# A summand for the fast matrix scheme, formed in place in its PSUM bank

## The chip, the core and the metric

The kernel runs on one core of a Trainium2 chip. Its engines work side by side: TensorE (PE; its weight loads are listed apart as PEld), VectorE (DVE), ScalarE (ACT) and GpSimd (POOL); SyncE issues the DMAs. Each engine executes its own queue in order, and waits for other engines by semaphores. The metric is the device time of one execution in microseconds (us).

## The reference

An attention layer is followed by two feed-forward layers (the setup of the inputs is left out):

```python
def _attn_ref(q, k, v, w1, b1, w2):          # q, k, v: 2 x 8 x 576 x 64
    ...
    scores = scale * np.matmul(q, k.transpose(0, 1, 3, 2))
    ...
    scores = scores + bias.transpose(2, 0, 1)[None, :, :, :]
    attn = softmax(scores)                    # exp, and division by the row's sum
    return np.matmul(attn, v)

def _moe_ref(x, w_gate, w_val, w_out):        # x: 1152 x 512, d_ff 1536
    g = x @ w_gate
    return (silu(g) * (x @ w_val)) @ w_out

def _moe2_ref(x, w_in, w_out):                # d_ff 2048
    return softplus(x @ w_in) @ w_out
```

The bias comes from a small network on the distance of two positions. All is float32.

## The kernel before

**Precision.** Products with full precision are made from two parts: a tensor's high part h is its value rounded to TensorE's format fp32r, its low part l is what is left (value minus h). Tiles with h or l at the end of the name are such parts.

**The feed-forward layers** (from line 640) multiply 2 x 2 blocks by a scheme with seven products instead of eight. The right-hand factor is the attention output, transposed and cut into blocks by head pairs and batches: B11 (head pairs 0 and 1, batch 0), B12 (the same, batch 1), B21 and B22 (head pairs 2 and 3). The scheme wants, beside the blocks, four sums: T1 = B12 − B11, T2 = B22 − T1, T3 = B22 − B12 and T4 = B21 − T2. All of them are kept as h and l.

**The attention** is done in eight units, one for each head pair and batch, in the order of `UNITS`: B11, B12 for head pair 0, B11, B12 for head pair 1, then B22 and B21. A unit has two parts (`sub`): the first with 256 query rows, the second with 320. A part has four or five chunks of scores. The function `run_slot` issues one chunk per slot, in a fixed order on all engines: TensorE makes the scores of the chunk (`scores`, tile ps, two buffers); finished parts are entered in a list (`finish`); copies of transposed blocks are made (`gather`, line 412, tiles at from pt); VectorE adds the bias to the scores and finds the row minima (`biased`, line 354); ScalarE takes the exp of the chunk before (`softmax`, line 368), VectorE sums and inverts (lines 372 and 375) and GpSimd scales (line 378); then pending preparations of queries and keys go on (`prep`, lines 189 to 195: h and l of Q and K, tiles qh, ql, kst); then `advance(late)` carries every finished part one step on; then TensorE transposes blocks (line 405). When all blocks of a part are copied, its value products run (`values`, line 432) in one go at the end of a slot, and the part is finished from the next slot on. They accumulate in the tile po, one PSUM bank; its pool has a single buffer:

```python
psO = pool("psO", 1, space=PSUM)     # line 622
```

**The end of a part** is the generator `finish` (line 440). Every `yield` without a value puts it off by a slot; `yield BLOCK` puts it off until the next part has issued its value products. For B12 it reads: ScalarE copies po to b12 (line 463); VectorE subtracts the high part of B11 from po into t1f, a place in SBUF that the bias no longer needs (line 464, by the helper of line 452, which is the line that the profile shows for every subtraction); behind a BLOCK, VectorE subtracts the low part of B11 from t1f, in place (line 466); a slot later ScalarE rounds t1f to T1h (line 468); behind one or two more BLOCKs VectorE makes T1l from t1f and T1h (line 472). t1f and b12 are read later, when B22 is finished (lines 476 and 477). So B12 goes through four such ends, two parts for each of the head pairs 0 and 1. In the trace, t1f and b12 carry the name bias, since they lie in a tile of the bias.

Of the kernel before, what the change touches and what calls it, by code (L numbers as in the profile page):

```python
# [44 lines left out]
BLOCK = "block"  # L45
# [58 lines left out]
def tile_kernel(ctx: ExitStack, tc, qT, kT, vS, vT, wg, wv, wo, wi, wo2, table, out):  # L104
    nc = tc.nc
# [11 lines left out]
    def slots(pool, tag, names):  # L117

        for name in names:
            n = len([1 for t in SLOTS.values() if t[0] == tag])  # L120
            SLOTS[name] = (tag, [pool.tile([P, 2, S], F32R, tag=f"{tag}{2 * n + i}", name=f"{name}{t}") for i, t in enumerate("hl")])

    def opener(stack):
        return lambda name, bufs, **k: stack.enter_context(
            tc.tile_pool(name=name, bufs=bufs, reuse_waits="tile", **k)
        )

    rctx = ExitStack()
    with ExitStack() as actx:
# [310 lines left out]
        def finish(u):  # L440

            if u["i"] == 2 and u["sub"] == 0:
                slots(xp, "a", ("B21", "B22"))
            if u["i"] == 4 and u["sub"] == 0:
                right.close()
                SLOTS["rp8"] = (None, opener(rctx)("rp8", 1, side="right"))
                slots(SLOTS["rp8"][1], "r", ("T2", "T3", "T4"))
            pr, sub, po = u["pr"], u["sub"], u["po"]
            n = 320 if sub else 256
            cols = slice(256 * sub, 256 * sub + n)  # L450
            po = po[:, :n]
            minus = lambda o, a, b, eng=nc.vector: eng.tensor_tensor(o, a, b, op=ALU.subtract)  # L452
            at = lambda name: [t[:, pr % 2, cols] for t in SLOTS[name][1]]
            floats = lambda name: [t.bitcast(F32) for t in at(name)]
            name = f"B{1 + pr // 2}{1 + u['b']}"
            if name != "B12":
                nc.scalar.copy(at(name)[0], po)
            k = pr % 2
            home = bias[1][:, 2 * k : 2 * k + 2, cols]
            t1f, b12 = home[:, 0], home[:, 1]  # L460
            chains = []
            if name == "B12":
                nc.scalar.copy(b12, po)
                minus(t1f, po, floats("B11")[0])
                yield BLOCK
                minus(t1f, t1f, floats("B11")[1])
                yield
                nc.scalar.copy(at("T1")[0], t1f)
                yield BLOCK
                if sub:  # L470
                    yield BLOCK
                minus(at("T1")[1], t1f, floats("T1")[0])
                return
            elif name == "B22":
                t2, t3 = t2f[:, k, cols], tmpp.tile([P, 320], F32, name="t")[:, :n]
                minus(t2, po, t1f)
                minus(t3, po, b12)
                chains = [("T2", t2), ("T3", t3)]
            elif name == "B21":
                t4 = tmpp.tile([P, 320], F32, name="t")[:, :n]  # L480
                minus(t4, po, t2f[:, k, cols])
                chains = [("T4", t4)]
            if not u["eager"]:
                yield
            if name != "B12":
                minus(at(name)[1], po, floats(name)[0])
            if u["eager"]:
                yield
                yield
            for to, t in chains:  # L490
                nc.scalar.copy(at(to)[0], t)
                yield
                minus(at(to)[1], t, floats(to)[0], nc.vector if u["eager"] else nc.gpsimd)
# [27 lines left out]
        def run_slot():  # L521
# [31 lines left out]
            for w in done:  # L553
                w["eager"] = slot >= len(chunks) - 1
                late.append(finish(w))
                if w["eager"]:
                    next(late[-1])
# [103 lines left out]
    def as_float(n):  # L661


        x = cvp.tile([P, 2 * NK, P], F32, tag="x", name="x")
        load(2 * n + 3)
        for j in range(2):
            raw, y = loaded[2 * n + j], x[:, NK * j : NK * (j + 1)]
            hw, lw, yi = raw[:, :, :, 1], raw[:, :, :, 0], y.bitcast(I32)
            if n < NL2:
                nc.scalar.activation(y, hw.bitcast(F32), AF.Prelu, scale=2.0**-112, alpha=-(2.0**32))  # L670
            else:
                nc.scalar.activation(y, hw.bitcast(F32), AF.Copy, scale=2.0**-112)  # L672
            nc.vector.tensor_scalar(yi, yi, 3, None, op0=ALU.logical_shift_left)  # L673
            if n >= NL2:
                nc.vector.scalar_tensor_tensor(yi, hw, -(2**31), yi, op0=ALU.bitwise_and, op1=ALU.bitwise_or)
            nc.vector.scalar_tensor_tensor(yi, lw, 29, yi, op0=ALU.logical_shift_right, op1=ALU.bitwise_or)  # L676
            load(2 * n + j + 4)
        return x
# [38 lines left out]
    class Quad:  # L717
# [8 lines left out]
        def floats(self):  # L726
            self.x = as_float(self.n)
# [129 lines left out]
    with tc.manual_schedule(engines={E.PE}):  # L857
# [118 lines left out]
        for m, order in ((2, (0, 1, 2)), (3, (2, 0, 1))):  # L976
            pt = [wide()[:, 0] for _ in TB]
            for fbs in [order[:1], order[1:]] if m == 3 else [(fb,) for fb in order]:
                at = {fb: blocks.index((m, fb)) for fb in fbs}
# [171 lines left out]
```

## Time and profile before

| | |
|---|---|
| Time, median of 3 runs | 587.55 us (587.5 to 587.6) |
| Profiled execution, span from first to last instruction | 585.8 us |
| Mean granted clock of TensorE | 1.000 of full speed |
| TensorE busy | 575.7 us (98%) |
| VectorE busy | 454.2 us (78%) |
| ScalarE busy | 374.8 us (64%) |
| GpSimd busy | 98.4 us (17%) |
| Line 452 on VectorE, second subtraction (bias<-bias,B11l) | 4 instructions, 81.5 to 130.0 us |
| Line 452 on VectorE, T1l | 4 instructions, 91.6 to 146.6 us |

The profiled execution's own time is given by its span alone. The attention fills the stretch from about 60 to 186 us; bias and first scores stand ahead of it, the feed-forward layers behind it. Times in a timeline are counted from the first instruction. A "part" below is one part of a unit as above; what is behind it in brackets in a row is the engine's idle time and the instruction that ended it, as far as the semaphores tell.

### The profile page before, as it was taken

What the parts mean: (1) busy time and instruction counts of PE and PEld (TensorE: products, weight loads), DVE (VectorE), ACT (ScalarE), POOL (GpSimd) and SP (SyncE); (2) the same over time, 40 slices, a digit from 0 to 9 for tenths busy, and PEclk for the clock granted to TensorE, in tenths of its full rate; (3) what the DMA queues carried; (4) which work ended last, traced back from release to release, by engine and by line L of the source; (5) the groups of instructions that cost most, each with busy time, mean ns of one, the idle gap of its engine ahead of it and who ended that gap; (6) DMA issues with size and microseconds to landing.
All of it is one profiled execution on the core that took longest, in us unless ns stands there. A gap on an engine that the chain in (4) does not pass through costs nothing.

```text
span 585.8 us, 11304 instructions
## 1 busy us (share of the span) xinstructions
PE 575.7 (98%) x4270; PEld 506.2 (86%) x4270; DVE 454.2 (78%) x970; ACT 374.8 (64%) x713; POOL 98.4 (17%) x151
## 2 busy tenths in 40 slices
PE   8999999999999999999999999999999999999997
PEld 5334588888887999999999999999989989989985
DVE  7999688888988998977879626579998877974332
ACT  8999888888787857656568325359727715733610
POOL 1002578888861000000000000000000000000000
PEclk9999999999999999999999999999999999999999
DMA  8999633233233342332343231322243241300012
GB/s 312 208 208 221 153 94 128 81 107 112 72 115 113 99 143 74 108 109 73 108 130 124 75 113 46 106 94 73 83 162 117 73 143 38 108 36 1 2 62 99
DMA packets 41894, 63.30 MB, mean 108 GB/s; under 512 B 4080, under 2 KB 30704, under 8 KB 41840
## 3 DMA queue, kind: packets, MB, share of 16 engines
q1 hardware_dynamic: 41840, 62.59, 36.1%
q8 instruction: 33, 0.54, 0.4%
q14 instruction: 21, 0.17, 0.1%
HBM read 49.60 MB, written 2.36 MB: 89 GB/s over the span
## 4 chain that ended last, share of the span: by engine, by line
PE 83%; DVE 7%; ACT 5%; DMA 3%; POOL 1%; issue 1%; DVEq 0%; ACTq 0%; POOLq 0%
PE pw L751 38%; PE pw L1059 17%; PE pw L702 13%; PE po L432 5%; PE pt L405 4%; PE ps L333 4%; DMA bias<-early 2%; PE ps L306 2%; ACT r L260 1%; PE pb L270 1%; ACT early L282 1%; DVE e L354 1%; DVE r L262 1%; DVE bias L354 1%; DVE T1l L452 1%
## 5 line engine op out<-in xcount | busy, mean ns | idle before, releaser
L1059 PE MATMUL pw<-oh,g2h 128*128 128x512 f32 x144 | 56.2, 390 | 0.0
L1059 PE MATMUL pw<-oh,g2l 128*128 128x512 f32 x144 | 56.2, 390 | 0.0
L1059 PE MATMUL pw<-ol,g2h 128*128 128x512 f32 x144 | 56.1, 390 | 0.0
L702 PE MATMUL pw<-gl,sh 128*128 128x384 f32 x144 | 48.2, 335 | 0.0
L702 PE MATMUL pw<-gh,sl 128*128 128x384 f32 x144 | 48.2, 334 | 0.0
L702 PE MATMUL pw<-gh,sh 128*128 128x384 f32 x144 | 48.2, 334 | 0.0
L262 DVE TENSOR_SCALAR r<-G 128x576 f32<-128x576 f32 x108 | 47.2, 522 | 0.1
L676 DVE SCALAR_TENSOR_TENSOR x<-raw,x 128x512 int32<-128x512 int32 x68 | 46.3, 688 | 0.9
L270 PE MATMUL pb<-r,G 128*32 128x288 f32 x576 | 44.4, 414 | 2.1
L378 POOL TENSOR_SCALAR e<-e,sm 128x576 f32<-128x576 f32 x44 | 33.8, 776 | 65.7 <-DVE sm L375 59.2
L270 PEld LDWEIGHTS pb<-r,G 128*32 128x32 f32 x576 | 18.8, 110 | 26.8 <-ACT early L282 15.1
L354 DVE CUSTOM_DVE_ANT_0 e<-ps,bias 128x576 f32<-128x576 f32 x44 | 33.0, 750 | 11.4 <-PE ps L333 6.6
L412 ACT COPY at<-pt 128x512 f32<-128x512 f32 (+2 forms) x69 | 36.4, 548 | 6.5 <-PE pt L405 6.1
L333 PE MATMUL ps<-kst,ql 128*128 128x288 f32 x120 | 36.9, 336 | 1.4 <-DVE sm L372 0.7
L432 PE MATMUL po<-at,v 128*64 128x256 f32 (+3 forms) x384 | 37.3, 332 | 1.0 <-DVE at L412 0.8
L1097 DVE TENSOR_TENSOR acc<-pw,acc 128x512 f32<-128x512 f32 x27 | 17.5, 685 | 25.1 <-PE pw L1059 25.1
L368 ACT ACTIVATE e<-e,sm 128x576 f32<-128x576 f32 x44 | 34.3, 781 | 3.5 <-DVE sm L354 3.0
L673 DVE TENSOR_SCALAR x<-x 128x512 int32<-128x512 int32 x68 | 28.8, 428 | 9.7 <-ACT x L672 5.0
L432 PEld LDWEIGHTS po<-at,v 128*64 128x64 f32 x384 | 26.8, 137 | 8.5 <-issue 1.7
L1059 PEld LDWEIGHTS pw<-oh,g2l 128*128 128x128 f32 x144 | 27.0, 188 | 5.8
L333 PE MATMUL ps<-kst,qh 128*128 128x288 f32 x120 | 32.0, 295 | 0.0
L681 ACT CAST oh<-x 128x512 fp32r<-128x512 f32 x16 | 9.9, 619 | 34.1 <-PE pw L1059 33.7
(270 smaller groups left out, 1684.3 us busy)
## 6 DMA issues: line engine op xcount, KB each, us to landing
raw<-in_wo_dram SPq DMA_DIRECT2D x28, 512.0 KB, 3.4
bias<-early SPq DMA_DIRECT2D x32, 288.0 KB, 8.1
raw<-in_wi_dram SPq DMA_DIRECT2D x16, 512.0 KB, 4.1
raw<-in_wv_dram SPq DMA_DIRECT2D x12, 512.0 KB, 4.6
raw<-in_wg_dram SPq DMA_DIRECT2D x12, 512.0 KB, 3.5
qr<-in_qT_dram SPq DMA_DIRECT2D x7, 576.0 KB, 3.7
bias<-in_kT_dram SPq DMA_DIRECT2D x6, 576.0 KB, 4.4
v<-in_vS_dram SPq DMA_DIRECT2D x8, 384.0 KB, 3.2
```

Source lines behind the costliest of these rows:

```text
L262: nc.vector.tensor_scalar(r, G[:, w0 : w0 + S], PB[:, n : n + 1], 0.0, op0=ALU.add, op1=ALU.max)
L270: nc.tensor.matmul(pb[32 * ct : 32 * ct + 32, hf, :HALF], W2, rs[ct][:, HALF * hf : HALF * (hf + 1)], start=True, stop=True,)
L333: nc.tensor.matmul(ps[:, hf, :HALF], u[t][:, o : o + P], kst[:, a, HALF * hf : HALF * (hf + 1)], start=i == 0, stop=i == len(parts) - 1,)
L354: nc.vector.tensor_tensor_reduce(out=e[:, :S].rearrange("p (a n) -> p a n", a=2), in0=ps[:, :, :HALF], in1=bt.rearrange("p (a n) -> p a n" ...
L368: nc.scalar.activation(e, e, AF.Exp, bias=sm[:, 0, n : n + 1], scale=-1.0, accum_out=u["sums"][:, n, :1])
L378: nc.gpsimd.tensor_scalar(e, e, sm[:, 2, i : i + 1], 1.0, op0=ALU.mult, op1=ALU.mult)
L412: marks[eng, u["i"], u["sub"]] = copy(at[:, :w], pt[:, :w]).ins
L432: nc.tensor.matmul(u["po"][D * a : D * (a + 1), o : o + n], v[:, D * t : D * (t + 1)], at[:, i : i + n], start=piece == 0 and o == 0, stop ...
L676: nc.vector.scalar_tensor_tensor(yi, lw, 29, yi, op0=ALU.logical_shift_right, op1=ALU.bitwise_or)
L702: nc.tensor.matmul(ps[:, :n], w[:, k], x, start=first and k == 0 and i == 0, stop=last and k == NK - 1 and i == 2)
L751: nc.tensor.matmul(ps[:, hf, :HALF], a[:, o + k], b[:, HALF * hf : HALF * (hf + 1)], start=start and k == 0 and i == 0, stop=k == 1 and i ...
L1059: nc.tensor.matmul(ps, g, w.rearrange("p k f -> p (k f)"), start=f == 0 and i == 0, stop=f == 3 and i == 2)
```

## The change

For B12 both subtractions of B11 now write their result back into po. They are made in two successive slots, without a BLOCK. Directly behind the second one ScalarE makes two copies out of po: T1h and the plain sum t1f. In the slot after that VectorE makes T1l from po and T1h. VectorE has as many subtractions as before; ScalarE has one copy more for each end, four in all.

```diff
@@ -460,16 +460,15 @@
             t1f, b12 = home[:, 0], home[:, 1]
             chains = []
             if name == "B12":
+                high11, low11 = floats("B11")
                 nc.scalar.copy(b12, po)
-                minus(t1f, po, floats("B11")[0])
-                yield BLOCK
-                minus(t1f, t1f, floats("B11")[1])
+                minus(po, po, high11)
                 yield
-                nc.scalar.copy(at("T1")[0], t1f)
-                yield BLOCK
-                if sub:
-                    yield BLOCK
-                minus(at("T1")[1], t1f, floats("T1")[0])
+                minus(po, po, low11)
+                nc.scalar.copy(at("T1")[0], po)
+                nc.scalar.copy(t1f, po)
+                yield
+                minus(at("T1")[1], po, floats("T1")[0])
                 return
```

The order of the instructions on VectorE and ScalarE moves with it; TensorE's does not.

VectorE, end of B12's second part for head pair 1, from the slot behind the one with the first subtraction; bias_72 holds t1f, bias_71 to bias_84 elsewhere are bias tiles or exp tiles, sm and sums the row statistics. Before:

```order
L372 TENSOR_REDUCE sm_101<-sums_105 128x1
L375 RECIPROCAL sm_101<-sm_101 128x1
L191 CAST qh<-qr 128x320
L412 COPY at<-pt 128x512
L354 ISA bias_82,sm_102<-ps,bias_71 128x576
L354 ISA sm_102 128x1
L372 TENSOR_REDUCE sm_102<-sums_106 128x1
L375 RECIPROCAL sm_102<-sm_102 128x1
L354 ISA bias_83,sm_102<-ps,bias_72 128x576
L354 ISA sm_102 128x1
L452 TENSOR_TENSOR T1l<-bias_72,T1h 128x256
L452 TENSOR_TENSOR bias_72<-bias_72,B11l 128x320
```

The two subtractions at the end stand a slot behind the value products; T1l (128x256) belongs to the part before. After:

```order
L372 TENSOR_REDUCE sm_101<-sums_105 128x1
L375 RECIPROCAL sm_101<-sm_101 128x1
L191 CAST qh<-qr 128x320
L452 TENSOR_TENSOR po<-po,B11l 128x320
L412 COPY at<-pt 128x512
L354 ISA bias_82,sm_102<-ps,bias_71 128x576
L354 ISA sm_102 128x1
L372 TENSOR_REDUCE sm_102<-sums_106 128x1
L375 RECIPROCAL sm_102<-sm_102 128x1
L452 TENSOR_TENSOR T1l<-po,T1h 128x320
L354 ISA bias_83,sm_102<-ps,bias_72 128x576
```

The second subtraction (128x320) has moved up to stand ahead of the copy of line 412, and T1l of the same part stands behind the next sum and reciprocal.

ScalarE, the same place, from the plain copy of po on; T1h is the high part of T1, at a copy of a transposed block. Before:

```order
L463 COPY bias_72<-po 128x320
L412 COPY at<-pt 128x512 x2
L368 ACTIVATE e_116,sums_105<-e_116,sm_101 128x576
L368 ACTIVATE bias_82,sums_106<-bias_82,sm_102 128x576
L189 CAST qh<-qr 128x320
L412 COPY at<-pt 128x256
L368 ACTIVATE bias_82,sums_106<-bias_82,sm_102 128x576
L412 COPY at<-pt 128x512
L368 ACTIVATE bias_83,sums_106<-bias_83,sm_102 128x576
L468 CAST T1h<-bias_72 128x320
```

Six instructions stand between the exp of e_116 and T1h. After:

```order
L464 COPY bias_72<-po 128x320
L412 COPY at<-pt 128x512 x2
L368 ACTIVATE e_116,sums_105<-e_116,sm_101 128x576
L468 CAST T1h<-po 128x320
L469 COPY bias_72<-po 128x320
L368 ACTIVATE bias_82,sums_106<-bias_82,sm_102 128x576
L189 CAST qh<-qr 128x320
L412 COPY at<-pt 128x256
L368 ACTIVATE bias_82,sums_106<-bias_82,sm_102 128x576
```

T1h and the plain sum stand directly behind that exp, ahead of the exp of bias_82 and the cast of the queries.

VectorE, end of B12's first part for head pair 1; kst are the parts of K of the next unit. Before:

```order
L191 CAST kst<-bias_71 128x576
L354 ISA e_115,sm_101<-ps,bias_82 128x576
L354 ISA sm_101 128x1
L195 TENSOR_TENSOR kst<-bias_71,kst 64x288
L412 COPY at<-pt 128x512
```

Neither the second subtraction nor T1l of this part stands here; they come later. After:

```order
L191 CAST kst<-bias_71 128x576
L452 TENSOR_TENSOR po<-po,B11l 128x256
L354 ISA e_115,sm_101<-ps,bias_82 128x576
L354 ISA sm_101 128x1
L195 TENSOR_TENSOR kst<-bias_71,kst 64x288
L452 TENSOR_TENSOR T1l<-po,T1h 128x256
L412 COPY at<-pt 128x512
```

The second subtraction stands behind the cast of K, T1l behind the subtraction of line 195.

## Rows read from the trace of the kernel before

**Rows 1.** Busy us by stretch: PE, PEld, DVE, ACT, POOL; clock, DMA share, GB/s.

```profile
90.00:130.00 40.00, 40.00 (x371) 35.03 (x366) 32.78 (x109) 33.36 (x82) 33.49 (x50) 1.00 0.35 108
130.00:170.00 40.00, 38.66 (x323) 32.71 (x321) 35.46 (x102) 33.23 (x83) 34.52 (x49) 1.00 0.33 107
```

**Rows 2.** Timeline, TensorE: start, length (us), line, operation, tiles.

```profile
80.06 2.45 PE L432 MATMUL po<-at,v 128*64 128x320 f32 x31
...
96.66 1.95 PE L432 MATMUL po<-at,v 128*64 128x256 f32 x16
...
120.52 2.45 PE L432 MATMUL po<-at,v 128*64 128x320 f32 x31
...
127.84 1.95 PE L432 MATMUL po<-at,v 128*64 128x256 f32 x16
```

**Rows 3.** Timeline, TensorE's weight loads; idle before in brackets.

```profile
112.33 1.49 PEld L432 LDWEIGHTS po<-at,v 128*64 128x64 f32 x16 [0.17 <-DVE B11l L452]
```

**Rows 4.** Timeline, VectorE, from A to E.

```profile
76.34 0.74 DVE L354 CUSTOM_DVE_ANT_0 e<-ps,bias 128x576 f32<-128x576 f32 x1
...
78.02 0.76 DVE L354 CUSTOM_DVE_ANT_0 e<-ps,bias 128x576 f32<-128x576 f32 x1 [0.65 <-PE ps L333]
...
94.16 0.47 DVE L452 TENSOR_TENSOR bias<-po,B11h 128x320 f32<-128x320 f32 x1
...
118.38 0.74 DVE L354 CUSTOM_DVE_ANT_0 e<-ps,bias 128x576 f32<-128x576 f32 x1
...
119.64 0.65 DVE L195 TENSOR_TENSOR kst<-bias,kst 64x288 fp32r<-64x288 f32 x1 [0.50 <-ACT kst L189]
...
125.35 0.47 DVE L452 TENSOR_TENSOR bias<-po,B11h 128x320 f32<-128x320 f32 x1
...
127.25 0.68 DVE L412 COPY at<-pt 128x512 f32<-128x512 f32 x1
...
128.52 0.15 DVE L372 TENSOR_REDUCE sm<-sums 128x1 f32<-128x2 f32 x1
...
128.79 0.74 DVE L354 CUSTOM_DVE_ANT_0 bias<-ps,bias 128x576 f32<-128x576 f32 x1
...
146.57 3.40 DVE L452 TENSOR_TENSOR T1l<-bias,T1h 128x320 fp32r<-128x320 f32 x1
```

**Rows 5.** Timeline, ScalarE, at A, C and D.

```profile
75.49 0.58 ACT L412 COPY at<-pt 128x512 f32<-128x512 f32 x1
...
117.22 1.06 ACT L412 COPY at<-pt 128x512 f32<-128x512 f32 x2
...
118.93 0.67 ACT L189 CAST kst<-bias 128x576 fp32r<-128x576 f32 x1
...
124.15 0.42 ACT L463 COPY bias<-po 128x320 f32<-128x320 f32 x1
...
126.62 0.77 ACT L368 ACTIVATE bias<-bias,sm 128x576 f32<-128x576 f32 x1
...
127.28 0.20 ACT L368 ACTIVATION_READ_ACCUMULATOR bias<-bias,sm 128x1 f32 x1
```

**Rows 6.** Line 452 by form: durations in ns (min/median/max), first and last start.

```profile
L452 DVE TENSOR_TENSOR bias<-po,B11h x4: 404/444/470, 74.7 to 125.3; 128x256 f32<-128x256 f32 x2, 128x320 f32<-128x320 f32 x2
L452 DVE TENSOR_TENSOR bias<-bias,B11l x4: 406/790/1159, 81.5 to 130.0; 128x256 f32<-128x256 f32 x2, 128x320 f32<-128x320 f32 x2
L452 DVE TENSOR_TENSOR T1l<-bias,T1h x4: 411/636/3404, 91.6 to 146.6; 128x256 fp32r<-128x256 f32 x2, 128x320 fp32r<-128x320 f32 x2
```

**Rows 7.** Timeline, TensorE, scores at A and behind E.

```profile
78.92 0.38 PE L333 MATMUL ps<-kst,ql 128*128 128x288 f32 x1
...
150.80 0.37 PE L333 MATMUL ps<-kst,ql 128*128 128x288 f32 x1 [0.65 <-DVE sm L372]
...
152.30 0.54 PE L333 MATMUL ps<-kst,ql 128*128 128x288 f32 x2 [0.30 <-DVE sm L354]
```

**Rows 8.** Timeline, GpSimd, end of a run at E.

```profile
148.76 0.87 POOL L452 TENSOR_TENSOR T3l<-t,T3h 128x320 fp32r<-128x320 f32 x1
```

## Prediction

> **What bounds the kernel now.** I read first the busy shares by stretch, to see which engine is full where the change works (60 to 150 us); then TensorE's rows there, to see when each value product starts; then the rows of VectorE and ScalarE from the moment a sum T1 begins until the next value product; last the waits. Between 90 and 130 us TensorE is busy 40.00 of 40 us at a granted clock of 1.00, while VectorE and ScalarE have a sixth of the time free; from 130 to 170 us it idles 1.34 us [rows 1]. So TensorE sets the time here. An instruction added to VectorE or ScalarE costs nothing by itself; whatever makes TensorE stand still costs its whole length, for the feed-forward part behind keeps TensorE full as well.
>
> The value products accumulate in `po`, and its pool has one buffer. The first value product of a part therefore waits for the last reader of `po` of the part before. Before, that reader is the first subtraction (and ScalarE's plain copy). After, it is the third, T1l. The question is where T1l stands against the start of the next value product.
>
> Four parts form T1: A and B (first and second part of head pair 0, batch 1), C and D (the same of head pair 1). E is the long T1l of D, which runs late at 146.57 us. After A to D the next value products start in the trace at 80.06 (A), 96.66 (B), 120.52 (C) and 127.84 (D) [rows 2].
>
> **How little room there is.** A row of before shows it. For a second part of a B11 block, the bank's last reader is B11l, which stands one slot behind the slot in which the part is finished. The next value product's weight load, at 112.33, was idle for 0.17 us, put down to that B11l [rows 3]. So one slot later is only just in time. After the change the second subtraction takes that slot and T1l comes one slot later still.
>
> **D, step by step.** The first subtraction stays at 125.35 [rows 4]. The second stands ahead of the copy that now starts at 127.25; with the 0.47 of the first subtraction it ends at 127.72 [rows 4]. ScalarE's T1h copy needs its result and now stands directly behind the exp of the slot, ahead of the exp that ran at 126.62. It waits until 127.72. T1h and the added second copy both read `po` and both take 0.42, as the plain copy of 124.15 does: 128.56 [rows 5]. The exp, from its start at 126.62 to the end of its accumulator read at 127.28 + 0.20, took 0.86 [rows 5]; it now ends at 129.42. VectorE's sum of 128.52 waits for that exp; from it to the instruction behind the reciprocal is 0.27 (128.52 to 128.79) [rows 4]. There T1l now stands: 129.69 to 130.16. The value product starts at 130.16 instead of 127.84: **+2.32 us**. What waits behind T1h on ScalarE is two exps, a cast and the copy for the last value piece; behind T1l on VectorE, the next biased scores.
>
> Bounds for D: if ScalarE's delay did not reach T1l, T1l would only be moved by the second subtraction, 128.79 + 0.47 + 0.47 = 129.73, +1.89. Less has no reason, since VectorE's order is fixed. I take 2.32, as VectorE's sum needs the delayed exp.
>
> **B** is the same code with the same neighbours: first subtraction at 94.16, value product at 96.66, 2.50 us apart against 2.49 in D [rows 2, 4]. I take **+2.3**, with the same bounds.
>
> **C** (256 columns). The second subtraction goes in front of the scores of 118.38 and takes 0.41, the shortest of its kind [rows 4, 6]: 118.79. T1h and the second copy, at 0.42 each, end by 119.63; that is where the two copies of 117.22 now begin, 2.41 later [rows 5]. The K cast of 118.93 moves to 121.34, and with its 0.67 ends at 122.01 [rows 5]. VectorE's K subtraction, at 119.64 before, waits for that cast; with its 0.65 it ends at 122.66, and T1l behind it at 123.07, against 120.52 [rows 2, 4]: +2.55. The 256-column copies should be shorter than the 320-column row that I used, so I take **+2.5**. Lower bound, ScalarE's delay not reaching it: 119.64 + 0.65 + 0.41 = 120.70, +0.2.
>
> **A** has most room (value product at 80.06 [rows 2]), and T1l is in time. But ScalarE's wait acts in another way. The second subtraction stands ahead of the scores of 76.34 and ends at 76.75 [rows 4]; T1h and the second copy end at 77.59. The copy of 75.49 [rows 5] now begins there; with its 0.58 and the 0.86 of the exp behind it this is 79.03. VectorE's sum waits for that exp; with the 0.27 from sum to next and T1l's 0.41 the scores of 78.02 start at 79.71 by whole durations. Neighbours on an engine overlap by about 0.1 us (the read of 127.28 begins before the exp's 126.62 + 0.77 is over [rows 5]), four times here: 79.3. Their 0.76 ends at about 80.1, and TensorE's scores of 78.92 need that score buffer (there are two) [rows 4, 7]: **+1.2**. Lower bound 0, if that exp is not held up; upper 1.6, without the overlaps.
>
> **E, a gain.** T1l of D, reading two SBUF operands, took 3.40 us, though its kind has a median of 0.64; the first subtraction, with `po` as an operand, never took over 0.47 [rows 6]. It ran from 146.57 to 149.97 [rows 4], and a run of GpSimd's instructions ended at 148.76 + 0.87 = 149.63 [rows 8]. Behind it TensorE waited 0.65 and 0.30 us for VectorE's scores [rows 7]. This instruction is gone from there, and its successor reads PSUM. I take **−0.95**, the two TensorE waits; bounds 0 and the excess itself, 3.40 − 0.47 = −2.93. The second subtractions get shorter too (median 0.79, against 0.44 of the first [rows 6]), but they run on VectorE in a stretch where it has a sixth of its time free [rows 1]: 0; were that cover gone, four times 0.35, −1.4.
>
> The Trainium skill, "SBUF — State Buffer", section "Who interferes with whom", says that a VectorE instruction with two SBUF inputs blocks against a GpSimd instruction that reads SBUF, and one with at most one such input does not. The 3.40 us row agrees. By that rule alone the change would be a gain; it is the faster rival below.
>
> **Sum:** 1.2 + 2.3 + 2.5 + 2.32 − 0.95 = +7.37. Nothing between D and the end has idle time of that size to take it back: TensorE idles 1.34 us in the 40 us behind D [rows 1], partly the two waits already counted. The profiled span is 585.8; the median of the timed runs, 587.55, is 1.75 above it, which the change does not touch. 585.8 + 7.37 + 1.75 = 594.92: I predict 594.9.
>
> **Rivals.**
> - *Only the bank, not ScalarE, holds up TensorE.* T1h finds its operand ready, because VectorE runs ahead. Then A 0, B 1.89, C 0.2, D 1.89, E −0.95: +3.0, 590.6. For it: ScalarE had idle stretches to make up. Against it: T1h stands one subtraction behind, with only one exp between.
> - *Faster.* The long T1l is the whole story, and the bank is free in time: −0.95, at most −2.93, so 586.6 to 584.6. Decided by whether T1l ends before the value products of B, C and D. For it: 3.40 us is the largest single stall. Against it: B11l is only just in time, one slot earlier than T1l will be [rows 3].
> - *Same.* The delays are real on VectorE and ScalarE but fill idle time later, or E repays up to its bound: 587.55 ± 1.2. Against it: 40.00 of 40.
> - *Larger.* Shifted instructions on VectorE meet GpSimd's runs elsewhere, as T1l did: 2.93 more for one such meeting, 597.8 and above. For it: the K subtractions keep two SBUF operands.
>
> **Chances.** Forecast (592.5 to 597.5) 0.66; only the bank (588.8 to 592.5) 0.14; larger 0.08; same 0.06; faster 0.06. The bounds give +1.05 at the least (0 + 1.89 + 0.2 + 1.89 − 2.93) and about +8.8 at the most (1.6 + 2.32 + 2.55 + 2.32 − 0). The range 589.2 to 598.0 holds the forecast and nearly all of the only-the-bank case, and leaves out the same, the faster and most of the larger: 0.19. Changes under 0.2% (1.2 us) cannot be told from none: slower 0.88, same 0.06, faster 0.06.
>
> **What would show it.** In the changed profile: weight loads of the value products behind B, C and D that sit idle about 2.4 us with T1l named as releaser; behind A no such wait, but one of about 1 us in front of scores; an idle ScalarE in front of T1h of about a microsecond, put down to the subtraction on `po`; no `T1l` over 0.5 us; TensorE's busy time unchanged with the span longer by the waits. I am wrong if those weight loads start where they did, or if TensorE's waits are there and the span is not longer.

## The result, and the profile after

The changed kernel takes 595.26 us (median of 4 runs, 595.13 to 595.33), the kernel before 587.58 in the same comparison: ratio 1.0129, 95% interval 1.0117 to 1.0141. 594.9 was predicted, in a range of 589.2 to 598.0. The profiled span is 593.5 us against 585.8, with a granted clock of 0.997. TensorE's busy time is 576.2 us against 575.7: it has no more work, it stands still for longer. In the comparisons of the experiments below, the kernel before took 587.4 to 588.1 us, and 586.4 in two of its 45 runs, of which no trace was kept.

TensorE's timeline of the changed kernel at the places of [rows 2] (start, length in us, line, operation, tiles; in brackets the idle time before and what ended it):

```profile
80.00 0.40 PE L333 MATMUL ps<-kst,ql 128*128 128x288 f32 x1 [0.36 <-DVE sm L354]
...
81.18 2.45 PE L432 MATMUL po<-at,v 128*64 128x320 f32 x31
...
100.03 1.95 PE L432 MATMUL po<-at,v 128*64 128x256 f32 x16 [2.21 <-DVE T1l L452]
...
123.40 0.44 PE L405 MATMUL pt<-ident,e 128*128 128x128 f32 x2 [0.72 <-ACT at L412]
...
126.15 2.45 PE L432 MATMUL po<-at,v 128*64 128x320 f32 x31 [1.24 <-DVE T1l L452]
...
135.76 2.48 PE L432 MATMUL po<-at,v 128*64 128x256 f32 x16 [2.20 <-DVE T1l L452]
```

The value products behind A, B, C and D start at 81.18, 100.03, 126.15 and 135.76 instead of 80.06, 96.66, 120.52 and 127.84. The trace runs 0.13 us early ahead of A, so the four parts add 1.25, 2.25, 2.25 and 2.29 us. In the last three TensorE waits for T1l, at C for a good half of the delay. The list of TensorE's waits (us in total, times, longest) sums these three, and has the one for ScalarE at C:

```profile
PE po L432 <- DVE T1l L452: 5.6, 3, 2.2
PE pt L405 <- ACT at L412: 0.7, 1, 0.7
```

The weight loads, which run ahead of their products, show the same stops, with the idle time in brackets:

```profile
77.86 0.42 PEld L405 LDWEIGHTS pt<-ident,e 128*128 128x128 f32 x4 [0.36 <-ACT at L412]
79.09 0.20 PEld L405 LDWEIGHTS pt<-ident,e 128*128 128x128 f32 x2 [0.29 <-ACT at L412]
80.00 0.19 PEld L333 LDWEIGHTS ps<-kst,ql 128*128 128x128 f32 x1 [0.60 <-DVE sm L354]
...
123.39 0.20 PEld L405 LDWEIGHTS pt<-ident,e 128*128 128x128 f32 x2 [0.95 <-ACT at L412]
126.15 2.10 PEld L432 LDWEIGHTS po<-at,v 128*64 128x64 f32 x30 [1.48 <-DVE T1l L452]
...
135.76 1.28 PEld L432 LDWEIGHTS po<-at,v 128*64 128x64 f32 x14 [2.44 <-DVE T1l L452]
```

At A there is no wait for the bank. Three short ones, 0.36 + 0.29 + 0.60 = 1.25, come from ScalarE's copies and from VectorE's scores. At C the 2.43 is shared by a ScalarE copy (0.95) and T1l (1.48). At D all 2.44 is T1l. Of the 2.43 and the 2.44, 0.17 are no delay: in the kernel before, such a load has as much in front of it where it waits for nothing, as behind D:

```profile
127.84 1.49 PEld L432 LDWEIGHTS po<-at,v 128*64 128x64 f32 x16 [0.17 <-issue]
```

That leaves 2.26 and 2.27, which is what the starts of the products show (2.25 and 2.29).

ScalarE at A and D, answering to [rows 5]:

```profile
76.67 0.37 ACT L468 CAST T1h<-po 128x256 fp32r<-128x256 f32 x1 [1.23 <-DVE po L452]
...
133.41 0.42 ACT L468 CAST T1h<-po 128x320 fp32r<-128x320 f32 x1 [1.05 <-DVE po L452]
133.74 0.43 ACT L469 COPY bias<-po 128x320 f32<-128x320 f32 x1
```

VectorE at D, answering to [rows 4]:

```profile
130.98 0.48 DVE L452 TENSOR_TENSOR po<-po,B11h 128x320 f32<-128x320 f32 x1
...
132.89 0.49 DVE L452 TENSOR_TENSOR po<-po,B11l 128x320 f32<-128x320 f32 x1
...
134.96 0.15 DVE L372 TENSOR_REDUCE sm<-sums 128x1 f32<-128x2 f32 x1 [0.32 <-ACT bias L368]
135.15 0.17 DVE L375 RECIPROCAL sm<-sm 128x1 f32<-128x1 f32 x1
135.23 0.47 DVE L452 TENSOR_TENSOR T1l<-po,T1h 128x320 fp32r<-128x320 f32 x1
```

Read the two together: the second subtraction ends at 133.38, T1h starts at 133.41 after 1.05 us of standing still, the exp behind the two copies is late, VectorE's sum at 134.96 waits 0.32 for it, T1l follows, and the product starts at 135.76. That is the predicted chain, link by link.

Line 452 by form (ns, min/median/max), answering to [rows 6]:

```profile
L452 DVE TENSOR_TENSOR po<-po,B11h x4: 412/452/479, 74.6 to 131.0; 128x256 f32<-128x256 f32 x2, 128x320 f32<-128x320 f32 x2
L452 DVE TENSOR_TENSOR po<-po,B11l x4: 414/454/493, 76.2 to 132.9; 128x256 f32<-128x256 f32 x2, 128x320 f32<-128x320 f32 x2
L452 DVE TENSOR_TENSOR T1l<-po,T1h x4: 405/448/473, 78.9 to 135.2; 128x256 fp32r<-128x256 f32 x2, 128x320 fp32r<-128x320 f32 x2
```

No T1l is over 0.473 us. VectorE's busy time falls by 5.3 us (448.9 against 454.2), and the time rises all the same.

Two things happen behind D. From 127.84 to 155.10 of the trace before, TensorE wins back 0.79 us net (the product of 155.10 starts at 162.23, 7.13 later); the prediction had a gain there, of 0.95. And its granted clock falls, which the prediction did not have, as busy time by stretch shows (PE, PEld, DVE, ACT, POOL, then the clock, DMA share, GB/s):

```profile
134.00:136.00 2.00, 0.24 (x2) 0.20 (x4) 1.65 (x6) 2.00 (x6) 1.17 (x2) 1.00 0.24 97
136.00:137.00 1.00, 1.00 (x12) 0.68 (x10) 0.38 (x2) 1.00 (x4) 1.00 (x2) 1.00 0.00 0
137.00:138.00 1.00, 1.00 (x8) 0.53 (x6) 0.00 (x0) 0.56 (x2) 0.07 (x1) 0.52 0.00 0
138.00:139.00 1.00, 1.00 (x6) 0.24 (x2) 0.00 (x0) 0.00 (x0) 0.00 (x0) 0.50 0.80 212
139.00:140.00 1.00, 1.00 (x6) 0.98 (x5) 0.00 (x0) 0.38 (x1) 0.00 (x0) 0.50 0.83 341
140.00:141.00 1.00, 1.00 (x9) 0.98 (x7) 0.62 (x1) 0.01 (x1) 0.00 (x0) 0.77 0.09 37
141.00:142.00 1.00, 1.00 (x11) 1.00 (x10) 0.97 (x7) 1.00 (x2) 0.41 (x1) 1.00 0.00 0
```

TensorE stands still for 2.20 us, starts again at 135.76, and from 137 to 140 has the lower of its two levels, half of full speed (1.2 GHz). So a loss and a larger gain lie on top of each other here, and the experiments have to part them.

### The profile page after: what moved, and what is told of

It reads as the page before. It is cut to its first block, busy times and chain, and to the rows that moved or that the text cites. A ratio compares the mean times of both kernels' runs of the same rounds, so it can differ in the third digit from the quotient of the medians.

```text
span 593.5 us, 11309 instructions
## 1 busy us (share of the span) xinstructions
PE 576.2 (97%) x4270; PEld 504.8 (85%) x4270; DVE 448.9 (76%) x970; ACT 375.7 (63%) x717; POOL 97.8 (16%) x151
## 4 chain that ended last, share of the span: by engine, by line
PE 81%; DVE 7%; ACT 7%; issue 2%; POOL 1%; DMA 1%; ACTq 0%; POOLq 0%; DVEq 0%
PE pw L750 37%; PE pw L1058 17%; PE pw L701 10%; PE po L432 6%; PE ps L333 3%; PE pt L405 3%; PE pb L270 2%; ACT early L282 2%; PE ps L306 1%; DMA bias<-early 1%; ACT r L260 1%; DVE e L354 1%; ACT at L412 1%; ACT e L368 1%; PE warm L596 1%
## 5 line engine op out<-in xcount | busy, mean ns | idle before, releaser
L270 PEld LDWEIGHTS pb<-r,G 128*32 128x32 f32 x576 | 16.6, 110 | 28.9 <-ACT early L282 16.0
L405 PE MATMUL pt<-ident,e 128*128 128x128 f32 x188 | 32.0, 278 | 1.0 <-ACT at L412 0.7
```

The source lines that it names most:

```text
L270: nc.tensor.matmul(pb[32 * ct : 32 * ct + 32, hf, :HALF], W2, rs[ct][:, HALF * hf : HALF * (hf + 1)], start=True, stop=True,)
L405: nc.tensor.transpose(pt[:, P * w : P * (w + 1)], e, ident)
```

## The experiments

All but the pair with a second bank are told by the same measure, read from the starts of the value products against those of before: what is added at A, B, C and D, and what the stretch behind D, up to the product of 155.10, adds or gives back. Figures with * hold a fall of the clock. Times are medians.

| kernel | A | B | C | D | behind D | time, us | ratio (95%) |
|---|---|---|---|---|---|---|---|
| changed | +1.25 | +2.25 | +2.25 | +2.29 | −0.79* | 595.26 | 1.0117 to 1.0141 |
| fill_bd | +1.25 | +2.26 | +2.26 | +2.29 | −2.45 | 593.53 | 1.0081 to 1.0115 |
| fill_d, its run of 595.09 us | +1.24 | +3.83* | +2.26 | +2.29 | −2.46 | 594.34 | 1.01 to 1.013 |
| first_parts | +1.23 | 0 | +2.25 | 0 | −2.25 | 588.81 | 1.0011 to 1.0029 |
| second_parts | 0 | +3.95* | 0 | +2.28 | −2.49 | 591.35 | 1.004 to 1.007 |
| t1l_sbuf | +1.24 | +0.71 | +0.96 | +1.92 | −2.49 | 590.25 | 1.003 to 1.0063 |
| one_slot | +0.08 | +0.39 | +0.31 | +0.40 | −2.50 | 586.37 | 0.9971 to 0.999 |
| late_t1l | +0.09 | +0.38 | +0.06 | +0.79 | −2.23 | 586.74 | 0.9974 to 0.9993 |
| before_pause | 0 | 0 | 0 | +2.34 | −2.25 | 587.77 | 0.9991 to 1.001 |

**Only the first parts (A, C), or only the second (B, D).** The B12 branch of the changed kernel under `if sub:`, the old one for the other parts (and the reverse for first_parts):

```diff
             if name == "B12":
                 nc.scalar.copy(b12, po)
+                if sub:                  # first_parts: if not sub:
+                    high11, low11 = floats("B11")
+                    minus(po, po, high11)
+                    yield
+                    ...
+                    minus(at("T1")[1], po, floats("T1")[0])
+                    return
```

> Only the first parts (A and C, 256 columns) are done in the changed way, B and D as before. Theory (each part has its own price: A 1.25 by ScalarE's hold, C 2.25 by hold and bank, the long T1l of D stays): 587.6 + 3.5 = 591.1 us (590.5 to 591.8). Rival (only the second parts cost, because only there the next value product comes four slots later): 588.8 or less.

> Only the second parts (B and D, 320 columns) are done in the changed way, A and C as before. Theory of a price per part: B 2.25, D 2.3, and behind D either the slow clock (1.4) with a gain of 2.2 where the long T1l was, or neither dip nor more than 0.95 of that gain: 587.6 + 3.7 = 591.3 us (590.6 to 592). If the clock falls behind D here too, C's wait is not what brings it down. Rival (waits repay each other because VectorE and ScalarE catch up during a stop): less than 590.

The prices stand part by part, whether the other parts are changed or not: A 1.23, C 2.25, D 2.28, and B 2.26 at the start of its product. first_parts came out at 588.81, the time of the rival and not 591.1. The rival's reason is wrong all the same, for A and C do cost their price; but the gain behind D is there in full although D, with the long T1l, keeps its old code. The second parts' T1l of that kernel, the line's instructions in ns (min/median/max):

```profile
L452 DVE TENSOR_TENSOR T1l<-bias,T1h x2: 661/668/675, 115.5 to 149.2; 128x320 fp32r<-128x320 f32 x2
```

The old T1l with two SBUF operands, at its old place in the program and 2.7 us later (149.2 against 146.57), takes 0.675 and not 3.40 us. So the predicted reason of the gain, T1l's removal, falls. In second_parts the clock fell at B: 0.50 from 99 to 102 us, and 1.68 us more is lost there. Three of its runs took 591.34 to 591.37 at a clock of 0.997, one took 589.84 at 1.000: 1.52 us for one fall.

**T1l from SBUF**, so that it is no longer the bank's last reader:

```diff
-                minus(at("T1")[1], po, floats("T1")[0])
+                minus(at("T1")[1], t1f, floats("T1")[0])
```

> As the changed kernel, but T1l reads the plain sum from SBUF instead of po, at the same place. Theory (bank): the bank is free with the second ScalarE copy, so the waits behind B, C and D shrink from 2.2 to about 0.7 us each (C 1.0 through the transposed blocks' copies that ScalarE makes late), A keeps 1.2, the long T1l stays away: 590.3 us (589 to 592). Rival (ScalarE's wait alone sets the loss, the bank's last reader does not matter): 594 or more.

590.25, as expected. Now ScalarE's second copy is the last reader, and the list of waits names it:

```profile
PE po L432 <- ACT bias L469: 1.2, 2, 0.7
PE pt L405 <- ACT at L412: 0.7, 1, 0.7
```

Up to the end of D the four parts add 1.24 + 0.71 + 0.96 + 1.92 = 4.83 (D's figure takes in 0.7 us within C's value product, 3.16 long against 2.45). So T1l as last reader of the bank is worth 8.04 − 4.83 = 3.2 of the 8.04 us. More than half remains without it: that is what the second subtraction's slot does through ScalarE.

**Both subtractions in one slot.** The `yield` stands behind both, T1h, the second copy and T1l follow in the next slot; and late_t1l, where T1l keeps its old place behind the BLOCKs and reads t1f in SBUF:

```diff
                 minus(po, po, high11)
-                yield
                 minus(po, po, low11)
+                yield
                 nc.scalar.copy(at("T1")[0], po)
                 nc.scalar.copy(t1f, po)
-                yield
                 minus(at("T1")[1], po, floats("T1")[0])
```

> Both subtractions in po stand in the first slot, the two ScalarE copies and T1l in the second. Theory (the loss is the slot in which T1l reads the bank, and ScalarE's wait for the second subtraction): T1h finds its operand ready, T1l ends where B11l ends for other blocks, just in time. Value products behind B, C and D start at most 0.3 us late, nothing at A, the long T1l is still gone: 587.0 us (586.2 to 588.2), against 587.6 before and 595.3 changed. Rival (the in-place writes into PSUM and the four added copies cost by themselves): at least 2 us remain, 589.6 or more.

> Both subtractions in po in the first slot, both ScalarE copies in the second, and T1l as late as in the kernel before, from SBUF. Theory (E: the long T1l costs TensorE 0.95 us): nothing lost at A to D, nothing gained at E: 587.7 us (587.2 to 588.2), about 0.9 slower than T1l from po in the second slot. Rival (the long T1l was hidden): equal to that kernel within 0.3.

one_slot takes 586.37, below both kernels: it loses 1.18 up to D and wins back 2.50 behind it. That gain is not owed to the slot; a mere pause brings it too, as before_pause shows below. At B, VectorE and ScalarE of this kernel:

```profile
94.20 0.48 DVE L452 TENSOR_TENSOR po<-po,B11h 128x320 f32<-128x320 f32 x1
94.71 0.50 DVE L452 TENSOR_TENSOR po<-po,B11l 128x320 f32<-128x320 f32 x1
...
96.28 0.48 DVE L452 TENSOR_TENSOR T1l<-po,T1h 128x320 fp32r<-128x320 f32 x1
```

```profile
95.46 0.42 ACT L468 CAST T1h<-po 128x320 fp32r<-128x320 f32 x1
95.77 0.45 ACT L469 COPY bias<-po 128x320 f32<-128x320 f32 x1
```

T1h has no idle time in front of it: its operand was ready at 95.21. T1l ends at 96.76, before the product (97.10), and TensorE has no wait for T1l at all. A to D cost 1.18 us together, against 8.04. The number of operations and the operands in PSUM are those of the changed kernel; only the slot differs. late_t1l was expected at 587.7, since a late T1l should have run long again, and came out at 586.74. Its longest T1l took 1.01 us: a miss that agrees with first_parts.

**A second bank for po**, taken from the three banks of pt, in the kernel before and in the changed one:

```diff
-            psT = pool("psT", 3, space=PSUM)
-            psO = pool("psO", 1, space=PSUM)
+            psT = pool("psT", 2, space=PSUM)
+            psO = pool("psO", 2, space=PSUM)
```

> The kernel before with two buffers of po and two of pt: the measure for the changed kernel with the same. A buffer of pt less should hold up transposes: 587.6 to 593 us, no theory told apart by its own time.

> The changed kernel with two buffers of po instead of one, and two of pt instead of three (PSUM has no bank more). Theory (bank): against the kernel before with the same buffers the change costs only ScalarE's hold, A 1.2 and C about 1, less 0.95 at E: +1.3 us (0 to 2.5). Rival (bank not the cause): +7.7 as with one buffer.

The kernel before takes 594.73 (1.0105 to 1.0135), above its expected 593, and the changed one 598.93 (1.0179 to 1.0209): 4.2 us apart, where 1.3 (0 to 2.5) was expected. TensorE's waits in the changed kernel with two banks:

```profile
PE pt L405 <- ACT at L412: 6.2, 8, 2.2
PE pt L405 <- DVE at L412: 5.9, 9, 0.9
```

In the kernel before with two banks the same two are 2.3 and 5.5. No wait for T1l is left, so the bank was the reason of those; but with a pt bank fewer, ScalarE's hold comes back as waits for pt. By the starts of the value products, the changed kernel loses 1.70, 0.38, 1.94 and 0.38 us more than the kernel before at A to D, and both have the same behind D (+0.11). So B and D cost 0.38 instead of 2.25 and 2.29 with a second bank, while A and C still cost 1.70 and 1.94, now as waits for ScalarE's copies. The pair's total is no price of the bank alone, since it holds the lack of the pt bank as well.

**The unchanged kernel with a pause.** Nine identity matmuls ahead of the value products behind D, nothing else:

```diff
                 u["po"] = psO.tile([P, 512], F32, name="po")
+                if u["i"] == 4 and u["sub"] == 0:
+                    fill = psT.tile([P, 512], F32, name="pt")
+                    for _ in range(9):
+                        nc.tensor.matmul(fill[:, :P], ident, ident, start=True, stop=True)
```

> The kernel before, unchanged, with nine identity matmuls put ahead of the value products behind D (their result is used by nothing). Six of them took 1.61 us in an earlier run, so nine are about 2.4 us of TensorE's time that moves everything behind D later, as the changed kernel does, with T1 still formed the old way. Theory (the collisions of VectorE with GpSimd behind D, the K subtraction of 1.70 us and the T1l of 3.40 us, belong to the phase in which the old timing puts them, and any shift dissolves them): the stretch from 136 to 156 us gives back about 2.2 to 2.5 us, the K subtraction and T1l are below 1.2 us each, and the time is 587.5, within 0.5 of before. Rival (what was gained there belongs to T1l's new place): nothing is given back, T1l stays near 3.4 us, and the time is 589.9.

587.77 against 587.71: the 2.34 us that were put in are given back, 2.25 of them before the product of 155.10. VectorE's row of the K subtraction behind D, in the trace of the kernel before, which the prediction does not name:

```profile
135.79 1.70 DVE L195 TENSOR_TENSOR kst<-bias,kst 64x288 fp32r<-64x288 f32 x1 [0.74 <-ACT kst L189]
```

and VectorE in the kernel with the pause, the same instruction and the T1l of D:

```profile
137.80 0.46 DVE L195 TENSOR_TENSOR kst<-bias,kst 64x288 fp32r<-64x288 f32 x1 [0.47 <-ACT kst L189]
...
148.13 0.67 DVE L456 TENSOR_TENSOR T1l<-bias,T1h 128x320 fp32r<-128x320 f32 x1
```

1.70 has become 0.46 and 3.40 has become 0.67, with nothing changed but the moment. From the second value product behind D to the third (136.26 to 145.21 before, 138.55 to 146.13 here) TensorE needs 1.37 us less, and from the third to the fourth (155.10, here 155.19) 0.83 less. The K subtraction stands at the head of the first of these stretches, T1l in the second.

**The stops filled.** The changed kernel with six such matmuls ahead of the value products behind D (fill_d), and behind B and D (fill_bd):

```diff
+                if u["i"] in (2, 4) and u["sub"] == 0:      # fill_d: u["i"] == 4
+                    fill = psT.tile([P, 512], F32, name="pt")
+                    for _ in range(6):
+                        nc.tensor.matmul(fill[:, :P], ident, ident, start=True, stop=True)
```

> As the changed kernel, with six matmuls of the identity on itself (results unused) in front of the value products behind D, where TensorE stood idle for 2.2 us and its granted clock was 0.50 from 137 to 140 us. They keep TensorE busy meanwhile. If the clock then stays at 1.00 and its loss adds to the rest: 1.4 us less, 593.9. If the slow stretch only took time that VectorE needed anyway: 595.1, within 0.3 of the changed kernel.

> The changed kernel with six identity matmuls ahead of the value products behind B and behind D, where TensorE stood idle for 2.2 us each (their result is used by nothing). They take 1.6 us of the idle time and should move nothing. Theory (the granted clock falls once, behind one of the long stops, and costs about 1.5 us when it does): with both stops filled no stretch has a clock below 1.00, and the time is 593.7 in every run. Rival (the fall of the clock does not depend on these stops): a clock below 1.00 somewhere between 80 and 160 us, and 595.2 as in the changed kernel.

fill_d alone took 593.54, 593.59, 595.09 and 595.25: two runs without a fall of the clock (0.999) and two with one (0.996 and 0.997). In the profiled one it had moved from D to B, as the stretches show:

```profile
98.00:100.00 2.00, 0.00 (x0) 0.00 (x0) 1.64 (x7) 2.00 (x7) 1.17 (x5) 1.00 0.11 46
100.00:102.00 2.00, 1.89 (x14) 1.25 (x16) 0.73 (x3) 1.90 (x5) 1.42 (x2) 0.81 0.00 0
102.00:104.00 2.00, 2.00 (x10) 0.96 (x7) 0.00 (x0) 0.34 (x1) 0.00 (x0) 0.50 0.77 209
104.00:106.00 2.00, 2.00 (x16) 1.98 (x16) 1.11 (x5) 0.69 (x3) 0.00 (x0) 0.84 0.23 94
```

With both stops filled all four runs took 593.47 to 593.62 at 0.999 or 1.000, and the stretches at B and D have the full clock:

```profile
98.00:106.00 8.00, 7.52 (x62) 6.37 (x63) 4.90 (x17) 6.52 (x18) 4.12 (x8) 1.00 0.30 96
134.00:142.00 8.00, 7.77 (x64) 6.62 (x65) 5.04 (x20) 6.53 (x18) 4.01 (x6) 1.00 0.25 79
```

The matmuls move nothing, A to D cost what they cost in the changed kernel, and 1.7 us are saved. So the fall of the clock follows one of the long stops, and costs 1.5 to 1.7 us.

## Why the prediction came out

The time was met because the four large terms were right, and because two errors nearly cancel: the gain behind D is 1.5 us larger than in the sum, and the fall of the clock, 1.5 to 1.7 us, is not in it. That these two cancel is luck. Without the fall the time is 593.5 (fill_bd), 1.4 below the number, though still within 592.5 to 597.5.

- **A, +1.2: right** (1.25; first_parts 1.23). The mechanism is the one told, ScalarE's hold: 1.23 us idle in front of T1h. It reached TensorE in three pieces, not in one wait of about 1 us. The scores of 78.92 start at 80.00, 1.21 later by the same measure, as the sum has it; but two stops for ScalarE's copies, which it does not name, lie within that delay.
- **B and D, +2.3 and +2.32: right** (2.25 and 2.29). T1l is the releaser, with weight loads idle for 2.44 us, and the link over ScalarE holds: t1l_sbuf and one_slot show that the slot of the second subtraction is the root, and the bank's last reader one of two ways by which it reaches TensorE.
- **C, +2.5: right in mechanism, 0.25 too large.** The two copies of 256 columns take less than the 320-column row that was used (T1h 0.37 at A), which accounts for a part of it. Only a part of the delay is a wait for T1l, since a ScalarE copy takes the other.
- **E, −0.95: wrong in its reason, and too small,** though within its bound of −2.93. The step said that the long T1l "is gone from there, and its successor reads PSUM". before_pause and first_parts show that neither matters: the same instruction takes 0.67 us if its moment shifts. And there were two long instructions behind D, not one; the K subtraction of 1.70 us was missed. For T1l's stretch alone the 0.95 is near what before_pause wins there (0.83); the K subtraction's stretch gives 1.37. Without a fall of the clock the gain is −2.25 to −2.50 in every kernel of the table, whatever moved the phase.
- **Missed: the clock**, +1.5 to +1.7 for one long stop in a run.
- **"How little room there is": right, but read from a row that does not show it.** The idle time of 0.17 in [rows 3] stands in front of the loads at 80.06, 96.66, 120.52 and 127.84 too, where nothing was waited for. What carries the reading is the end of that B11l at 112.23, 0.10 ahead of the load of 112.33:

```profile
111.76 0.47 DVE L452 TENSOR_TENSOR B11l<-po,B11h 128x320 fp32r<-128x320 f32 x1
```

The sum by what was measured: 8.04 for A to D, −2.45 behind D (as in fill_bd) and 1.5 to 1.7 for the clock give 7.1 to 7.3 at the product of 155.10, where 7.26 is measured (7.13 and the offset of 0.13). The span is 7.7 longer. The first product behind the attention starts 7.21 later (193.51 against 186.30), so the last 0.5 arises in the feed-forward layers; its cause is open.

Of the rivals, "only the bank" failed at ScalarE: T1h did not find its operand ready. "Faster" had the right row, 3.40 us, but drew the whole forecast from it; the waits for T1l behind B, C and D decided against it. With the −2.3 of before_pause in place of the −0.95, the sum is 8.32 − 2.3 = 6.0, which gives 593.6: the time of fill_bd.

On the excess of those two instructions the Trainium skill, "SBUF — State Buffer", section "Who interferes with whom", says that a VectorE instruction with two SBUF inputs contends with a GpSimd instruction that reads SBUF. The long rows are of that kind, and the traces bear it out. Which of the two is held goes here by the order of their starts. GpSimd's rows beside the K subtraction, in the kernel before (where that ran from 135.79 to 137.49) and then in the one with the pause (137.80 to 138.26):

```profile
135.62 0.79 POOL L195 TENSOR_TENSOR kst<-bias,kst 64x288 fp32r<-64x288 f32 x1
136.38 0.79 POOL L195 TENSOR_TENSOR kst<-bias,kst 64x288 fp32r<-64x288 f32 x1
```

```profile
137.89 1.03 POOL L195 TENSOR_TENSOR kst<-bias,kst 64x288 fp32r<-64x288 f32 x1
```

Before, the K subtraction starts 0.17 us behind the first of these rows and ends 0.32 behind the end of the second (137.17). With the pause it starts 0.09 ahead of GpSimd's row and takes its 0.46, and GpSimd takes 1.03 instead of 0.79. The twelve traces of this document hold this instruction 72 times. In 53 of them it took 0.51 us or more; each of the 53 started while an instruction ran on GpSimd, and ended 0.31 to 0.38 behind the end of one. In the other 19, GpSimd ran nothing or had at most 0.06 left, and it took 0.46. The T1l of 3.40 us fits: it ended 0.34 behind the 149.63 of [rows 8]. So GpSimd held both instructions. What stays open is why VectorE did not get its turn at the first end that came (136.41 for the K subtraction, and three such ends for T1l).

## What to carry to other kernels

With an operand in PSUM no subtraction here took over 0.50 us, but every reader of a bank that has one buffer holds up the next accumulation: count the slots from the end of an accumulation to its last reader, and put all that reads the bank into the first of them that is possible. A copy on an engine that runs in order waits for its operand at the expense of all behind it, so place it by the slot in which the operand is ready, not by the slot in which it is wanted. Before a gain is booked for an instruction that runs long once, ask whether a shift by a microsecond or two would do the same: a pause in the old kernel is a cheap test.

## What the runs showed of the hardware

- One stop of TensorE of 2.2 us was followed by some 3 us at a granted clock of 0.50, at a cost of 1.5 to 1.7 us. The lower clock began about 1.3 us behind the restart in the changed kernel (135.76), and within 0.1 us of it in second_parts (98.92). The changed kernel has two such stops and its profiled run one fall (behind D, not behind B); fill_d's and second_parts' profiled runs have theirs behind B. Matmuls of no use in the stops kept the clock at 1.00 (fill_bd).
- A VectorE subtraction of two SBUF operands took 1.70 or 0.46 us, and another 3.40 or 0.67, in kernels that differ by 2.3 us of pause before it. The first took 1.14 in the changed kernel. Where such a K subtraction took longer than 0.46, in 53 rows of twelve traces, it ended 0.31 to 0.38 us behind the end of a GpSimd instruction.
- A stretch of TensorE that is counted as busy can hold a loss: from 136 to 146 us it idles 0.37 in the kernel before (9.63 of 10 busy), but with the pause the work from 136.26 to 145.21 takes 1.37 less. The rest of the loss lies within rows counted as busy, such as a value product of 2.76 us that takes 2.45 with the pause.
